# The 64-row products of an expansion placed beside the 64-row turns, whole-height state sums in the first group, and y times G on VectorE for the first two units

## The chip, the cores and the metric

The kernel runs on one core of a Trainium2 chip. The metric is the device time of one execution in microseconds. Before the change it is 840.27 us, the median of 3 runs (839.8 to 841.61); the profiled execution spans 840.4 us. All data are 32-bit floats.

## The reference

A linear-attention layer with a recurrent state is followed by a feed-forward block. The attention part runs over 4 batches x 8 heads x 768 steps with a head width of 40:

```python
for t in range(S):
    y[:, :, t] = einsum('bhd,bhde->bhe', r_t, state)
    Sa = einsum('bhde,bhe->bhd', state, a_t)
    state = state * w_t[:, :, None, :] - einsum('bhd,bhe->bhde', Sa, b_t) \
            + einsum('bhd,bhe->bhde', v_t, k_t)
```

Its output, read as 3072 tokens of width 320, goes through

```python
h = x @ w_in                      # 320 -> 2048
g = h * clip(h + 3, 0, 6) / 6
out = g @ w_out                   # 2048 -> 320
```

## The kernel before

The sequence is worked through in blocks of 64 steps. A *unit* is two batches of one such block, so there are 24 units; four units make a *group*. For each unit the kernel turns the inputs (transposes on TensorE), forms running products of the decay, solves a small triangular system (by an inverse that VectorE builds once a group, then small TensorE products), and updates the state: that is the scan. The finished output of a unit, `yg`, is moved by DMA into `xt`, laid out as two blocks of 128 features and one block of 64 features, the latter held twice, in rows 0 to 63 and in rows 64 to 127. The feed-forward block then runs on 128 tokens in two jobs per unit, each over half of the 2048 hidden features. In the first part of the run the 64-bit weights in HBM are also converted to 32 bits, by VectorE and ScalarE.

Programs of the engines are fixed when the kernel is built: a Python generator hands out the feed-forward work in *pieces*, which are put between the stages of the scan.

An expansion (320 features to 1024 hidden ones) fills two PSUM banks. Its first four pieces are products over 128 rows, and its fifth is the eight products over the last 64 features, in pairs that use rows 0 to 63 and rows 64 to 127:

```python
def expand(xt, j0, gts):
    hp = [bank("h", [P, NQ, P], 2) for _ in range(2)]
    for c in range(2):
        for t in range(2):
            for i in range(NQ):                                    # NQ = 4
                j = c * HJ + j0 + i
                nc.tensor.matmul(out=hp[c][:, i, :], lhsT=win[:, t, j * P:(j + 1) * P],   # L968
                                 rhs=xt[:, t, :], start=(t == 0 and i == 0), stop=False)
            yield True
    for i in range(NQ):
        for c in range(2):
            nc.tensor.matmul(out=hp[c][:, i, :],                                          # L973
                             lhsT=win2[half(c), (j0 + i) * P:(j0 + i + 1) * P],
                             rhs=xt[half(c), 2, :], start=False, stop=(i == NQ - 1))
    for c in range(2):
        gt = ffn.tile([P, NQ, P], F32, name="gt", bufs=5)
        nc.scalar.activation(out=gt[:], in_=hp[c][:], func=AF.Relu, ...)                  # L978
        nc.vector.scalar_tensor_tensor(out=gt[:], in0=gt[:], scalar=6.0, in1=hp[c][:], ...)  # L979
        gts.append(gt)
    yield True
```

The contraction of the job before follows in four pieces of two products each (16 of the profile's instructions in all), into one bank (`o`, L992). The generator alternates them:

```python
i, r = jobs.popleft()
gts = []
yield from expand(ready[i], r * NQ, gts)
if last:
    yield from contract(*last)
last = (i, r, gts)
```

The steady part of the scan issues the stages of several units together. `PRODUCTS` gives the order on TensorE: first the full 128-row turns `W`, `S`, `K`; then `RT`, `VT`, `A`, `B`, `factor`, which are *half turns* (64 rows by 128 columns, L430 and L570); then products on quarters of the array (64 rows by 64 columns):

```python
PRODUCTS = ["W", "S", "K", "RT", "VT", "A", "B", "factor",
            "y", "EV", "R", "C", "U", "UT", "rS", "sn", "H", "E", "F"]
TURNS = PRODUCTS[:3]
def together(stages):
    ...
    for name in PRODUCTS:
        for stage in stages.get(name, []):
            ...                       # the stage's TensorE part
    ...                               # then every stage's results
```

Two stages of the scan in detail. The new state is summed over 40 rows at a time, since a head has 40 rows in each half of the array:

```python
def s_sn():
    sn = ps_pair(NPR, D)
    ...
            nc.tensor.matmul(out=sn[q][half(s, D), pr, :],                                # L864
                             lhsT=o[name][half(q), h * D:(h + 1) * D], rhs=by, ...)
    yield PE
    for q in range(2):
        for s in range(2):
            x = st[half(s, D), q, :, 0:D]
            nc.vector.tensor_tensor(out=x, in0=sn[q][half(s, D)], in1=x, op=ALU.add)      # L873
```

The unit's output is multiplied by the running decay G. In the first two units (`fresh`: the state is still zero) there is nothing to add to it:

```python
def s_y():
    y = ps_pair(NPR, BL)
    ...                                                                                   # L888
    yield PE
    if fresh:
        m["ys"] = tmp.tile([P, NPR, 2, BL], F32, name="ys", tag="zs")
    for q in range(2):
        if fresh:
            nc.scalar.activation(out=m["ys"][:, :, q, :], in_=y[q], func=AF.Copy)         # L898
        else:
            nc.vector.tensor_tensor(out=m["ys"][:, :, q, :], in0=y[q],
                                    in1=m["ys"][:, :, q, :], op=ALU.add)                  # L900
    yg = m["yg"] = tmp.tile([P, NPR, P], F32, name="yg", tag="yg", bufs=2)
    nc.gpsimd.tensor_tensor(out=yg[:], in0=m["ys"]..., in1=o["G"][:], op=ALU.mult)        # L903
```

The tag `zs` is a single buffer; the triangular blocks (`third_block`) use it as well: ScalarE writes `zs` (L704) and TensorE reads it (L719).

Of the kernel before, what the change touches and what calls it, by code (L numbers as in the profile page):

```python
# [16 lines left out]
P = 128  # L17
BL = 64
HB = BL // 2
L = 32  # L20
SLOT = 64
# [8 lines left out]
def kernel(  # L30
# [42 lines left out]
    nc = tc.nc  # L73
    B, H, T, D = r.shape
    NG = T // (2 * BL)
    NPR = H // 2
    NP = B // 2
    NU = 2 * NP
# [16 lines left out]
    def bank(tag, shape, bufs):  # L95
        return ps.tile(shape, F32, name=tag, tag=tag, bufs=bufs)
# [11 lines left out]
    def ps_pair(*dims):  # L108

        n = 1  # L110
        for d in dims:
            n *= d
        if shared[0] is None or shared[1] + n > 512:
            shared[:] = [ps_any([P, 512]) for _ in range(2)], 0
        at = shared[1]
        shared[1] += n
        views, step = [], n
        for d in dims:
            step //= d
            views.append([step, d])  # L120
        return [_ap(t[:], at, views) for t in shared[0]]
# [6 lines left out]
        out=ident[:], in_=ones, pattern=[[1, P]],  # L128
# [4 lines left out]
        out=ones[:, 0:BL], in_=ones[:, 0:BL], pattern=[[1, BL]],  # L133
# [3 lines left out]
        out=ones[BL:P, 0:BL], in_=ones[BL:P, BL:P], pattern=[[1, BL]],  # L137
# [310 lines left out]
    def half(i, n=SLOT):  # L448
        return slice(SLOT * i, SLOT * i + n)
# [285 lines left out]
    def step(i):  # L735
# [117 lines left out]
                nc.scalar.activation(out=ys[:, rs::2], in_=ysp[rs], func=AF.Copy)  # L853

        def s_sn():
            sn = ps_pair(NPR, D)
            for name in "KB":
                for pr in range(NPR):
                    for s in range(2):
                        for q in range(2):  # L860
                            h = 2 * pr + s
                            by = VN[half(q), 4 * s + pr, 0:D] if name == "K" else \
                                m["U"][half(q), 4 * (s ^ q) + pr, 0:D]
                            nc.tensor.matmul(  # L864
                                out=sn[q][half(s, D), pr, :],
                                lhsT=o[name][half(q), h * D:(h + 1) * D], rhs=by,
                                start=(name == "K" and pr == 0), stop=(name == "B" and pr == NPR - 1),
                            )
# [11 lines left out]
        def s_y():  # L880
            y = ps_pair(NPR, BL)
            for name in "KB":
                for pr in range(NPR):
                    j, rs = pr // 2, pr % 2
                    for s in range(2):
                        for q in range(2):
                            h = 2 * pr + s
                            nc.tensor.matmul(  # L888
                                out=y[q][half(s), pr, :],
                                lhsT=o[name][half(q), h * D:h * D + SLOT],  # L890
                                rhs=m[name][half(q), 4 * rs + 2 * s + j, :],
                                start=(name == "K" and pr == 0), stop=(name == "B" and pr == NPR - 1))
            yield PE
            if fresh:
                m["ys"] = tmp.tile([P, NPR, 2, BL], F32, name="ys", tag="zs")
            for q in range(2):
                if fresh:
                    nc.scalar.activation(out=m["ys"][:, :, q, :], in_=y[q], func=AF.Copy)  # L898
                else:
                    nc.vector.tensor_tensor(out=m["ys"][:, :, q, :], in0=y[q],  # L900
                                            in1=m["ys"][:, :, q, :], op=ALU.add)
            yg = m["yg"] = tmp.tile([P, NPR, P], F32, name="yg", tag="yg", bufs=2)
            nc.gpsimd.tensor_tensor(out=yg[:], in0=m["ys"][:].rearrange("p r q t -> p r (q t)"),  # L903
                                    in1=o["G"][:], op=ALU.mult)

# [39 lines left out]
    def feed_forward():  # L945

        last = None
        while True:
            while not available():
                if last:  # L950
                    yield from contract(*last)
                    last = None
                yield None
            i, r = jobs.popleft()
            gts = []
            yield from expand(ready[i], r * NQ, gts)
            if last:
                yield from contract(*last)
            last = (i, r, gts)

    def expand(xt, j0, gts):

        hp = [bank("h", [P, NQ, P], 2) for _ in range(2)]
        for c in range(2):
            for t in range(2):
                for i in range(NQ):
                    j = c * HJ + j0 + i
                    nc.tensor.matmul(out=hp[c][:, i, :], lhsT=win[:, t, j * P:(j + 1) * P],  # L968
                                     rhs=xt[:, t, :], start=(t == 0 and i == 0), stop=False)
                yield True  # L970
        for i in range(NQ):
            for c in range(2):
                nc.tensor.matmul(out=hp[c][:, i, :],  # L973
                                 lhsT=win2[half(c), (j0 + i) * P:(j0 + i + 1) * P],
                                 rhs=xt[half(c), 2, :], start=False, stop=(i == NQ - 1))
        for c in range(2):
            gt = ffn.tile([P, NQ, P], F32, name="gt", bufs=5)
            nc.scalar.activation(out=gt[:], in_=hp[c][:], func=AF.Relu, bias=three[:], scale=1.0)  # L978
            nc.vector.scalar_tensor_tensor(out=gt[:], in0=gt[:], scalar=6.0, in1=hp[c][:],  # L979
                                           op0=ALU.min, op1=ALU.mult)  # L980
            gts.append(gt)
        yield True

    def contract(i, r, gts):
        split = i < SPLIT
# [292 lines left out]

    m = 0
    for i in range(NU, NK):  # L1280
        for j in range(BLOCKS):
            rate, inversion = 3.5, 0
            if i + AHEAD >= NK + NU - 1:
                rate = 4.5
            if i < 2 * NU - 1:
                rate = 2.8
            parts = a_block(m)
            next(parts)
            if side or i % NU == NU - 1 and rate < 4:
# [12 lines left out]
            m += 1  # L1302
# [36 lines left out]
```

## Time and profile before

| | |
|---|---|
| time, median of 3 | 840.27 us |
| TensorE (PE), matmuls | 753.9 us busy, 90% |
| VectorE (DVE) | 549.1 us, 65% |
| ScalarE (ACT) | 322.6 us, 38% |
| GpSimd (POOL) | 158.2 us, 19% |
| mean granted TensorE clock | 0.937 |
| PE busy, 330 to 760 us | 100, 99.02, 100 and 59.97 us in the stretches 400-500, 500-600, 600-700 and 700-760; 70 of 70 us in 330-400 |
| PE busy, 60 to 150 us | 33.55 of 60, then 20.99 of 30 us |
| DVE busy, 60 to 150 us | 47.99 of 60, then 23.56 of 30 us |

In the profile each 32-bit product stands as two TensorE instructions: the 768 products at L968 are 1536 there. They are pipelined and overlap, so what one costs is read from start to start, and not from its own duration. A form such as `64*128` gives the rows and columns of the array that an instruction uses.

### The profile page before, as it was taken

How to read it: one execution, taken by the hardware profiler on the slowest of the kernel's cores; microseconds unless marked ns; L12 is line 12 of the kernel's file. 1: busy time of each engine (PE TensorE's matmuls, PEld its weight loads, DVE VectorE, ACT ScalarE, POOL GpSimd, SP SyncE). 2: the span in 40 equal slices, each digit the busy share in tenths (PEclk: the TensorE clock that was granted, in tenths of full speed). 3: DMA queues.
4: the chain of work that ended last, by engine and by line, in shares of the span. 5: the costliest groups of instructions: out<-in, count | busy, mean ns of one | idle time of the engine just before them, and what ended most of it. 6: DMA issues, size and time to landing. Idle time of an engine off the chain costs nothing.

```text
span 840.4 us, 35835 instructions
## 1 busy us (share of the span) xinstructions
PE 753.9 (90%) x15832; PEld 635.5 (76%) x15832; DVE 549.1 (65%) x1112; ACT 322.6 (38%) x868; POOL 158.2 (19%) x307
## 2 busy tenths in 40 slices
PE   4722866898999998999999999999999999999998
PEld 3622766686877877888888888888888888888886
DVE  6989597887865769855589744699556675232211
ACT  1322654232265533454433545334553324322111
POOL 3231310222112230312230322022122102000000
PEclk9755576999999998999999999999999999999999
DMA  7573343331033331232321332231232101110000
GB/s 140 83 176 92 90 105 91 69 68 34 9 59 59 63 61 28 43 55 46 61 44 33 59 59 44 44 57 29 47 64 43 24 22 28 25 23 15 16 19 16
DMA packets 174218, 45.05 MB, mean 54 GB/s; under 512 B 157424, under 2 KB 172784, under 8 KB 174064
## 3 DMA queue, kind: packets, MB, share of 16 engines
q1 hardware_dynamic: 171920, 42.44, 25.7%
q8 instruction: 125, 2.05, 1.0%
q10 hardware_dynamic: 2144, 0.33, 0.2%
q14 instruction: 29, 0.24, 0.1%
HBM read 34.08 MB, written 3.93 MB: 45 GB/s over the span
## 4 chain that ended last, share of the span: by engine, by line
PE 73%; DVE 12%; issue 6%; ACT 2%; POOL 2%; DMA 2%; SPq 0%; POOLq 0%; DVEq 0%; ACTq 0%
PE o L992 23%; PE h L968 20%; PE h L973 5%; PE any L458 4%; PE any L888 3%; PE any L420 2%; PE any L430 2%; PE any L864 2%; PE any L770 1%; DVE prod L660 1%; PE any L809 1%; DVE parts L320 1%; DVE x L666 1%; PE any L830 1%; DVE score L467 1%
## 5 line engine op out<-in xcount | busy, mean ns | idle before, releaser
L992 PE MATMUL o<-wout,gt 128*128 128x320 f32 x768 | 234.6, 449 | 0.0
L968 PE MATMUL h<-xt,win 128*128 128x128 f32 x1536 | 198.1, 283 | 5.0 <-DVE gt L979 5.0
L968 PEld LDWEIGHTS h<-xt,win 128*128 128x128 f32 x1536 | 186.7, 196 | 13.9 <-DVE gt L979 5.7
L992 PEld LDWEIGHTS o<-wout,gt 128*128 128x128 f32 x768 | 139.3, 191 | 54.4 <-issue 1.4
L979 DVE SCALAR_TENSOR_TENSOR gt<-gt,h 128x512 f32<-128x512 f32 x96 | 61.3, 681 | 87.1 <-ACT gt L978 87.0
L978 ACT ACTIVATE gt<-h,three 128x512 f32<-128x512 f32 x96 | 60.8, 684 | 108.3 <-PE h L973 108.2
L903 POOL TENSOR_TENSOR yg<-ys,gam 128x512 f32<-128x512 f32 x24 | 41.4, 1726 | 182.9 <-DVE ys L900 125.5
L660 DVE TENSOR_TENSOR prod<-x 128x30 f32<-128x30 f32 (+9 forms) x180 | 61.9, 344 | 13.5 <-POOL x L651 8.1
L590 POOL TENSOR_TENSOR KBt<-K,rgt 128x320 f32<-128x320 f32 x24 | 21.2, 882 | 248.2 <-ACT rgt L580 213.2
L666 DVE TENSOR_TENSOR x<-x,prod 128x30 f32<-128x30 f32 (+9 forms) x180 | 63.3, 352 | 5.2
L873 DVE TENSOR_TENSOR state<-any,state 40x160 f32<-40x160 f32 x96 | 30.9, 321 | 47.5 <-PE any L458 26.0
L973 PE MATMUL h<-xt,win 64*128 64x128 f32 x768 | 55.8, 285 | 0.0
L467 DVE COPY_PREDICATED score<-mask,any 128x256 f32<-128x256 int32 x143 | 53.4, 437 | 1.7 <-PE any L458 1.1
L973 PEld LDWEIGHTS h<-xt,win 64*128 64x128 f32 x768 | 46.6, 187 | 5.2 <-issue 0.3
L495 DVE RECIPROCAL gam<-prods 128x256 f32<-128x256 f32 x24 | 41.5, 1741 | 13.4 <-POOL yg L903 12.1
L510 DVE RECIPROCAL rgam<-prods 128x256 f32<-128x256 f32 x24 | 41.8, 1741 | 0.0
L484 DVE TENSOR_TENSOR_SCAN prods<-wm,start 128x528 f32<-128x528 f32 x24 | 30.1, 1254 | 17.5 <-ACT wm L481 15.8
L623 ACT ACTIVATE EV<-any 64x160 f32<-64x160 f32 x92 | 24.9, 297 | 43.0 <-PE any L617 34.7
L888 PE MATMUL any<-score,KBt 64*64 64x64 f32 x1536 | 31.8, 233 | 3.5 <-DVE score L467 2.1
L888 PEld LDWEIGHTS any<-score,KBt 64*64 64x64 f32 x1536 | 27.9, 145 | 6.4 <-issue 2.4
L900 DVE TENSOR_TENSOR ys<-any,ys 128x256 f32<-128x256 f32 x44 | 16.6, 419 | 24.4 <-PE any L617 12.6
L749 ACT ACTIVATE RT<-any 128x256 f32<-128x256 f32 (+1 forms) x44 | 15.5, 401 | 42.4 <-PE any L430 42.4
(195 smaller groups left out, 1107.2 us busy)
## 6 DMA issues: line engine op xcount, KB each, us to landing
B<-in_b_dram SPq DMA_DIRECT2D x48, 80.0 KB
K<-in_k_dram SPq DMA_DIRECT2D x48, 80.0 KB
V<-in_v_dram SPq DMA_DIRECT2D x96, 40.0 KB
out_dram<-ob SPq DMA_DIRECT2D x48, 80.0 KB
R<-in_r_dram SPq DMA_DIRECT2D x92, 40.0 KB
W<-in_w_dram SPq DMA_DIRECT2D x40, 80.0 KB
A<-in_a_dram SPq DMA_DIRECT2D x40, 80.0 KB
xt<-yg SPq DMA_DIRECT2D x72, 40.0 KB
```

The source lines that it names most:

```text
L467: nc.vector.copy_predicated(out=x[:, 4 * i:4 * i + 4, :], mask=mask4, data=o[i])
L495: nc.vector.reciprocal(gv[:, :, 0:HB], o["prods"][:, :, 0, 1:HB + 1][:, :, ::-1])
L510: nc.vector.reciprocal(rv[:, :, HB:BL], o["prods"][:, :, 1, 1:HB + 1])
L660: nc.vector.tensor_tensor(out=pv, in0=_ap(x[:], (i + 1) * L + i, [[L, n], [0, i]]), in1=_ap(x[:], i * L, [[0, n], [1, i]]), op=ALU.mult,)
L666: nc.vector.tensor_tensor(out=rest, in0=rest, in1=pv, op=ALU.add)
L888: nc.tensor.matmul(out=y[q][half(s), pr, :], lhsT=o[name][half(q), h * D:h * D + SLOT], rhs=m[name][half(q), 4 * rs + 2 * s + j, :], start ...
L903: nc.gpsimd.tensor_tensor(out=yg[:], in0=m["ys"][:].rearrange("p r q t -> p r (q t)"), in1=o["G"][:], op=ALU.mult)
L968: nc.tensor.matmul(out=hp[c][:, i, :], lhsT=win[:, t, j * P:(j + 1) * P], rhs=xt[:, t, :], start=(t == 0 and i == 0), stop=False)
L973: nc.tensor.matmul(out=hp[c][:, i, :], lhsT=win2[half(c), (j0 + i) * P:(j0 + i + 1) * P], rhs=xt[half(c), 2, :], start=False, stop=(i == N ...
L978: nc.scalar.activation(out=gt[:], in_=hp[c][:], func=AF.Relu, bias=three[:], scale=1.0)
L979: nc.vector.scalar_tensor_tensor(out=gt[:], in0=gt[:], scalar=6.0, in1=hp[c][:], op0=ALU.min, op1=ALU.mult)
L992: nc.tensor.matmul(out=op[:], lhsT=gts[c][:, n, :], rhs=wout[:, c * HJ + r * NQ + n, :], start=((split or r == 0) and c == 0 and n == 0), ...
```

## The change

It has three parts.

1. The eight 64-row products of an expansion no longer have to be its fifth piece. From unit 7's turn on (`spread`), they are held back or drawn forward: `together` issues them ahead of the first half turn (or, where a stage has no half turn, ahead of the first of its narrow products). If no such place has come by then, they go out after the third piece of the contraction that follows. The results (L978, L979 before) are issued as soon as both the 128-row and the 64-row products have been. As an expansion is then four pieces instead of five, the rate of pieces is multiplied by 8/9.
2. In the first group (units 0 to 3), the state's products take 64 columns of the weights instead of 40, so that all 128 rows of `sn` are written, and VectorE adds two 128-row tiles instead of four 40-row ones. The extra rows are not used later.
3. For the first two units VectorE multiplies `y` by `G` straight from PSUM, in two instructions; ScalarE's two copies and GpSimd's multiplication go, and so does the use of the buffer `zs`.

```diff
         def s_sn():
+            wide = SLOT if i < NU else D
...
-                                out=sn[q][half(s, D), pr, :],
-                                lhsT=o[name][half(q), h * D:(h + 1) * D], rhs=by,
+                                out=sn[q][half(s, wide), pr, :],
+                                lhsT=o[name][half(q), h * D:h * D + wide], rhs=by,
...
-                for s in range(2):
-                    x = st[half(s, D), q, :, 0:D]
-                    nc.vector.tensor_tensor(out=x, in0=sn[q][half(s, D)], in1=x, op=ALU.add)
+                for rows in [slice(0, P)] if i < NU else [half(s, D) for s in range(2)]:
+                    x = st[rows, q, :, 0:D]
+                    nc.vector.tensor_tensor(out=x, in0=sn[q][rows], in1=x, op=ALU.add)
...
+            yg = m["yg"] = tmp.tile([P, NPR, P], F32, name="yg", tag="yg", bufs=2)
             if fresh:
-                m["ys"] = tmp.tile([P, NPR, 2, BL], F32, name="ys", tag="zs")
+                for q in range(2):
+                    nc.vector.tensor_tensor(out=yg[:, :, half(q)], in0=y[q], in1=o["G"][:, :, half(q)],
+                                            op=ALU.mult)
+                return
...
+    narrow, spread, LATEST = [], [False], 2
...
             if last:
-                yield from contract(*last)
+                for n, x in enumerate(contract(*last)):
+                    if n == LATEST and narrow:
+                        narrow[0]()
+                    yield x
+            if narrow:
+                narrow[0]()
...
+        def short():
+            narrow.clear()
+            for i in range(NQ):
+                for c in range(2):
+                    add(c, i, win2[half(c), (j0 + i) * P:(j0 + i + 1) * P], xt[half(c), 2, :])
+            if begun[0] + begun[1] == 6 * NQ:
+                results()
...
+        narrow.append(short)
         for c in range(2):
             for t in range(2):
                 for i in range(NQ):
...
+                if c == 1 and t == 1 and not narrow:
+                    results()
                 yield True
...
+        if not spread[0] and narrow:
+            short()
+            yield True
...
-        owed[0] += n
+        owed[0] += n * (8 / 9 if spread[0] else 1)
...
+    FIRST_NARROW = PRODUCTS[len(TURNS)]
...
         for name in PRODUCTS:
+            if name == FIRST_NARROW and narrow and spread[0] and stages:
+                narrow[0]()
...
     for i in range(NU, NK):
+        spread[0] = i >= 2 * NU - 1
```

More of the change, by code (lines that the diff above doesn't have):

```diff
@@ L893, in s_y @@
             yield PE
+            yg = m["yg"] = tmp.tile([P, NPR, P], F32, name="yg", tag="yg", bufs=2)
             if fresh:
-                m["ys"] = tmp.tile([P, NPR, 2, BL], F32, name="ys", tag="zs")
+                for q in range(2):
+                    nc.vector.tensor_tensor(out=yg[:, :, half(q)], in0=y[q], in1=o["G"][:, :, half(q)],
+                                            op=ALU.mult)
+                return
             for q in range(2):
[L897 to L902, printed above, removed]
+                nc.vector.tensor_tensor(out=m["ys"][:, :, q, :], in0=y[q],
+                                        in1=m["ys"][:, :, q, :], op=ALU.add)
             nc.gpsimd.tensor_tensor(out=yg[:], in0=m["ys"][:].rearrange("p r q t -> p r (q t)"),
@@ L963, in expand, with add, results @@
         hp = [bank("h", [P, NQ, P], 2) for _ in range(2)]
+        begun = [0, 0]
+        def add(c, i, lhsT, rhs):
+            nc.tensor.matmul(out=hp[c][:, i, :], lhsT=lhsT, rhs=rhs, start=(begun[c] == 0),
+                             stop=(begun[c] == 3 * NQ - 1))
+            begun[c] += 1
+        def short():
[5 more added lines that the diff above has]
+                results()
+        def results():
+            for c in range(2):
+                gt = ffn.tile([P, NQ, P], F32, name="gt", bufs=5)
+                nc.scalar.activation(out=gt[:], in_=hp[c][:], func=AF.Relu, bias=three[:], scale=1.0)
+                nc.vector.scalar_tensor_tensor(out=gt[:], in0=gt[:], scalar=6.0, in1=hp[c][:],
+                                               op0=ALU.min, op1=ALU.mult)
+                gts.append(gt)
+        narrow.append(short)
         for c in range(2):
@@ L967, in expand @@
                     j = c * HJ + j0 + i
-                    nc.tensor.matmul(out=hp[c][:, i, :], lhsT=win[:, t, j * P:(j + 1) * P],
-                                     rhs=xt[:, t, :], start=(t == 0 and i == 0), stop=False)
+                    add(c, i, win[:, t, j * P:(j + 1) * P], xt[:, t, :])
+                if c == 1 and t == 1 and not narrow:
+                    results()
                 yield True
[L971 to L982, printed above, removed]
+        if not spread[0] and narrow:
+            short()
+            yield True
     def contract(i, r, gts):
```

## The prediction

> **What bounds the kernel now.** I read the 40 slices first, then the chain that ended last, then windows of TensorE's timeline.
>
> ```profile
> PE   4722866898999998999999999999999999999998
> DVE  6989597887865769855589744699556675232211
> ...
> PE 73%; DVE 12%; issue 6%; ACT 2%; POOL 2%; DMA 2%; SPq 0%; POOLq 0%; DVEq 0%; ACTq 0%
> ```
>
> There are two regimes. Until about 157 us (slice 7) TensorE is half idle and VectorE is the fullest engine; from there TensorE is full to the end. Adding the gaps between its records gives 18.7 us of idle time from 88 to 157 us, 6.3 from 157 to 250, 5.5 from 250 to 330, and only 1.2 from 330 to 840. So after 330 us everything taken off TensorE's sequence comes off the time, and nothing done to another engine does. But "busy" there doesn't mean at its best rate, as the timeline of a stretch shows:
>
> ```profile
> 515.33 1.34 PE L992 MATMUL o<-wout,gt 128*128 128x320 f32 x4
> 516.51 1.95 PE L968 MATMUL h<-xt,win 128*128 128x128 f32 x16
> 518.30 0.60 PE L420 MATMUL any<-ident,W 128*128 128x128 f32 x4
> 518.83 0.47 PE L430 MATMUL any<-ident,R 64*128 64x64 f32 x8
> ...
> 521.01 2.05 PE L968 MATMUL h<-xt,win 128*128 128x128 f32 x16
> 523.00 1.16 PE L973 MATMUL h<-xt,win 64*128 64x128 f32 x16
> 524.09 1.34 PE L992 MATMUL o<-wout,gt 128*128 128x320 f32 x4
> ```
>
> Sixteen wide products from 516.51 to 518.30 take 1.79 us (0.112 each) when the neighbours on both sides use 128 rows. The sixteen from 521.01 to 523.00, between a narrow block and the 64-row products, take 1.99. The 0.2 us is in the switches: in the records of single instructions the first step inside is 213 ns and not 112, and the last one, to L973, 205. L973 likewise: pairs come 112 ns apart, but the first pair takes 213, the last product is 201 ns from L992 where 105 would do, and L992's first step is 374, not 269. The sum for 64-row products alone among wide ones is 93 + 101 + 96 + 105 = 0.39 us. The end of the run confirms it:
>
> ```profile
> 813.39 3.73 PE L968 MATMUL h<-xt,win 128*128 128x128 f32 x32
> 817.05 1.16 PE L973 MATMUL h<-xt,win 64*128 64x128 f32 x16
> 818.15 4.57 PE L992 MATMUL o<-wout,gt 128*128 128x320 f32 x16
> 822.56 3.73 PE L968 MATMUL h<-xt,win 128*128 128x128 f32 x32
> ```
>
> A job takes 822.56 - 813.39 = 9.17 us, while 32 x 0.112 + 8 x 0.112 + 16 x 0.269 is 8.78.
>
> **What the Trainium skill says.** "TensorEngine Tiling (Array Packing)", Key Properties: changing the tiling mode, not just the tile, drains TensorE. The trace agrees: each change between `128*128`, `64*128` and `64*64` costs about 0.1 us on either side. The records from wide to half turn give 94 + 50 ns, from half turn to quarter product 122 on the step, from quarter product back to wide 133 + 101 to 111. A full turn followed by a wide product of the same form keeps the 109 ns step: turning as such is no switch. "TensorE: Matmul & The Clock Gate", LDWEIGHTS: a weight load takes time by its columns, not its rows. Agrees: L864 with 40 columns steps by 10 ns, L809 with 64 and the same 40 moving elements by 14. "VectorE: DVE Perf Modes", First, the fixed hardware budget: each of the 128 partitions is a lane. So adding 128 rows should last as long as adding 40; the trace has no 128-row twin of L873, but L775, 128x160 from PSUM, took 316 ns against its 321.
>
> **Part 1, the 64-row products.** I counted neighbours in the order of TensorE's instructions in the two programs, 48 blocks each. Before, 33 stand alone among 128-row instructions, 12 follow quarter products and precede wide ones, and 3 precede quarter products. After, 27 stand directly ahead of half turns (15 behind a full turn, 10 behind wide products, 2 behind a contraction), 8 alone, 2 behind quarter products and 11 ahead of them. What one adds in switches:
> - alone: 0.39 us (0.35 where a full turn follows);
> - between quarter and wide products: 242 + 201 - 244 (the switch that is there anyway) = 0.20;
> - between wide and quarter products: 194 + about 130 - 115 = 0.21, where 130 is my estimate from the 122 of half turns to quarter products;
> - ahead of half turns: the entry costs 194, but the half turns no longer pay theirs of 144, and the step between the two is of one form, `64*128`. With 20 ns for that (a half turn to the next one steps by 29 above its pace), 0.07 us.
>
> Before: 33 x 0.38 + 12 x 0.20 + 3 x 0.21 = 15.6 us. After: 8 x 0.39 + 27 x 0.07 + 2 x 0.20 + 11 x 0.21 = 7.7. That takes off 8 us, nearly all of it after 290 us where TensorE is the bound. The arithmetic itself stays.
>
> **Its price.** With no stages left at the end, three blocks go out after the third contraction piece, and only four instructions (4 x 0.269 + 0.105 = 1.18 us) lie between them and the next use of what they release.
>
> ```profile
> 827.31 8.88 PE L992 MATMUL o<-wout,gt 128*128 128x320 f32 x32
> 827.41 1.27 ACT L978 ACTIVATE gt<-h,three 128x512 f32<-128x512 f32 x2 [4.17 <-PE h L973]
> 828.14 1.28 DVE L979 SCALAR_TENSOR_TENSOR gt<-gt,h 128x512 f32<-128x512 f32 x2 [7.88 <-ACT gt L978]
> ```
>
> The first bank is free at 828.14 + 0.64, which is 1.5 us after the 64-row products gave way at 827.31; TensorE waits some 0.35 us, three times: +1 us. In the scan, stages lie between the forced place and the next expansion, so I give later results only +0.7 us: the wait for L979 was 1.0 us in all after 330 us.
>
> **Parts 2 and 3, the start.** All four first state sums are pieces of the chain (90.1, 103.2, 126.6, 153.9 us). Each loses two of four adds: 4 x 2 x 0.321 = 2.6 us. The first y:
>
> ```profile
> 98.69 1.08 PE L719 MATMUL any<-zs,tt 32*32 32x32 f32 x64
> 99.92 0.66 ACT L898 ACTIVATE ys<-any 128x256 f32<-128x256 f32 x2 [2.87 <-PE any L719]
> 100.65 1.29 POOL L903 TENSOR_TENSOR yg<-ys,gam 128x512 f32<-128x512 f32 x1 [10.14 <-ACT ys L898]
> 101.89 0.21 POOL L755 TENSOR_TENSOR scale<-last,dec 128x8 f32<-128x8 f32 x1
> 102.14 0.49 DVE L757 TENSOR_TENSOR state<-state,scale 128x320 f32<-128x320 f32 x1 [4.37 <-POOL scale L755]
> ```
>
> The product y ended at 97.7, but ScalarE's copy waited for L719, a reader of the shared `zs` buffer; the small `scale` stood behind the long multiplication in GpSimd's queue, and VectorE waited 4.4 us for it. Afterwards VectorE multiplies at 97.7 (2 x 0.4 us, by L900's 419 ns), does L299 and L307 (0.36 + 0.61) and could scale the state at 99.6. The next state sum then waits for TensorE's L864, which no longer waits 0.6 us for the copies, and starts near 101.2 and not 103.15. The balance by 157 us: 1.9 here, 2.6 from the sums, -0.8 for the second unit's multiplication on VectorE, and -0.5 for wider weights (64 x 4 ns = 0.26 us a unit, partly on the path) = 3.2. I count 2.5, as parts of this chain run over ScalarE and a TensorE at half clock (0.56 granted from 60 to 120 us).
>
> **Sum.** 840.3 - 8.0 - 2.5 + 1.0 + 0.7 = 831.5 us.
>
> **Rivals.**
> *The step from 64-row products to half turns is a switch too.* The one is a multiplication, the other a transpose. For: no record before has this pair. Against: in the 128-row form the two mix at 109 ns. It would cost 27 x about 0.15 to 0.2 = 4 to 5 us of the 8: 836.
> *VectorE or a PSUM bank becomes the bound in the middle.* VectorE is 73% busy from 400 to 600 us and runs in order; each `gt` now stands ahead of a stage's results, 1.3 us of it, and a half turn comes 1.1 us later than before. Against: the scan's products after the turn (0.5 to 1.5 us) cover that, and TensorE waited 1.2 us in 510. If each of some 40 blocks lost 0.15 us, +6: 837.
> *The early gain is hidden.* From 198 to 320 us there are waits of several us behind the inverse and behind GpSimd's `KBt` and the loads that it releases. If these are timed by DMA and not by what TensorE finished, 2.5 us are lost: 834. They seem to hang on TensorE's order, so I leave half a chance.
>
> **Range and chances.** The first part is the largest and the best founded; its main uncertainty is the one unseen step, which only makes it worse. All going well is 828, two rivals at once 838. Range 827.5 to 837. Faster by over 2% would be below 823.5: 0.03. Slower by over 2%, above 857: 0.01.
>
> **What would show it.** Right: half turns 0.06 to 0.13 us behind the last 64-row product at full pace; wide runs closing at 112 ns more often; the block L973's mean step unchanged; after 330 us TensorE idle below 3 us, and that stretch about 7 us shorter; the state scaling near 99.6 us, with its 4.4 us wait gone; dense TensorE work beginning 2 to 3 us before 157. Wrong: a 0.2 us step from 64-row products to half turns; waits of L968 for `gt` growing past 3 us; the first job starting as late as before.

## The result and the profile after

| | before | after |
|---|---|---|
| time, median | 840.15 us (839.8 to 841.61, 4 runs) | 832.7 us (831.98 to 834.51, 4 runs) |
| ratio | | 0.9911, 95% interval 0.9892 to 0.9931 |
| span of the profiled execution | 840.4 us | 830.2 us |
| TensorE idle, 330 us to its last instruction | 1.0 us | 6.5 us |
| first wide product; first product of a contraction | 118.19; 151.71 us | 113.73; 145.75 us |

The change takes off 0.9%, 7.5 us, and 831.5 was predicted. The total is right by luck: the start gave twice what was forecast, and the 64-row products a quarter to a third of their forecast.

The slices and the chain that ended last, after:

```profile
PE   4732877898999999999999999999999999999997
DVE  7999697988964769844589654799556685232201
...
PE 70%; DVE 12%; issue 9%; ACT 3%; POOL 2%; DMA 1%; SPq 0%; POOLq 0%; DVEq 0%; ACTq 0%
```

The digits look as before, but TensorE's share of the chain has fallen from 73 to 70% and "issue" has risen from 6 to 9%: more of the chain is time in which an engine waits for nothing that the profile shows.

The step that no record of before had, in the timeline after:

```profile
422.20 1.16 PE L974 MATMUL h<-xt,win 64*128 64x128 f32 x16
423.20 0.41 PE L430 MATMUL any<-ident,R 64*128 64x64 f32 x8
423.44 0.42 PE L430 MATMUL any<-ident,V 64*128 64x64 f32 x8
423.79 1.16 PE L889 MATMUL any<-score,KBt 64*64 64x64 f32 x64
```

From 422.20 to 423.20 is 1.00 us: eight pairs at 0.112 and one entry of 0.10. Nothing is left for a switch to the half turns; multiplication and transpose of one form follow each other at full pace. (L974, L990, L1015 and L865 are the lines L968/L973, L979, L992 and L864 of before.)

The three longest entries among the waits of TensorE from 322 us on (us in all, times, the longest), after:

```profile
PE h L974 <- DVE gt L990: 2.7, 4, 1.2
PE any L458 <- issue: 2.1, 3, 0.8
PE any L696 <- ACT wm L481: 1.3, 1, 1.3
```

Before, the same view had a single line, `L968 <- DVE gt L979` with 1.0 us. This is where the gain of the middle went. The end of the run, after:

```profile
802.19 3.84 PE L974 MATMUL h<-xt,win 128*128 128x128 f32 x32 [0.22 <-DVE gt L990]
...
809.19 1.16 PE L974 MATMUL h<-xt,win 64*128 64x128 f32 x16
810.28 1.34 PE L1015 MATMUL o<-wout,gt 128*128 128x320 f32 x4
811.84 3.84 PE L974 MATMUL h<-xt,win 128*128 128x128 f32 x32 [0.22 <-DVE gt L990]
```

The wait for a free PSUM bank behind the forced place was foreseen; it shows as 0.22 us of idle time and comes three times. A job takes 811.84 - 802.19 = 9.65 us, though, where it took 9.17 before: 0.48 us more. Matmuls overlap (a contraction product lasts 0.53 us and the next one begins after 0.27), so the profile counts TensorE as busy until the last one ahead of a wait has run out, and its idle time is less than the delay. And the start, where before the state was scaled at 102.14 us, 12.04 us after the first state sum of 90.10, and the second sum began at 103.15:

```profile
96.09 0.76 DVE L898 TENSOR_TENSOR yg<-any,gam 128x256 f32<-128x256 f32 x2 [2.45 <-PE any L889]
97.70 0.48 DVE L757 TENSOR_TENSOR state<-state,scale 128x320 f32<-128x320 f32 x1
98.75 0.56 DVE L874 TENSOR_TENSOR state<-any,state 128x160 f32<-128x160 f32 x2
```

After, the first sum is at 89.36 us, so the scaling follows it by 8.34 and the second sum by 9.39 (13.05 before). VectorE's wait for GpSimd is gone. Counting from the first sum takes out the start of a program, which differs between the profiled executions (the first sum is at 89.36 us here and at 90.46 in gamlate, a kernel that has parts 2 and 3 too).

### The profile page after: what moved, and what is told of

It is laid out like the page before. It is cut to its first block, busy times and chain, and to the rows that moved or that the text cites. A ratio compares the mean times of both kernels' runs of the same rounds, so it can differ in the third digit from the quotient of the medians.

```text
span 830.2 us, 35843 instructions
## 1 busy us (share of the span) xinstructions
PE 746.4 (90%) x15832; PEld 632.0 (76%) x15832; DVE 547.4 (66%) x1108; ACT 321.7 (39%) x864; POOL 156.1 (19%) x305
## 3 DMA queue, kind: packets, MB, share of 16 engines
q8 instruction: 125, 2.05, 1.0%
## 4 chain that ended last, share of the span: by engine, by line
PE 70%; DVE 12%; issue 9%; ACT 3%; POOL 2%; DMA 1%; SPq 0%; POOLq 0%; DVEq 0%; ACTq 0%
PE h L974 24%; PE o L1015 22%; PE any L458 4%; PE any L889 3%; PE any L420 2%; PE any L430 2%; PE any L865 2%; DVE prod L660 2%; DVE x L666 2%; PE any L770 1%; PE any L809 1%; DVE parts L320 1%; PE any L830 1%; PE any L846 1%; PE any L696 1%
## 5 line engine op out<-in xcount | busy, mean ns | idle before, releaser
L974 PE MATMUL h<-xt,win 128*128 128x128 f32 (+1 forms) x2304 | 252.8, 284 | 7.0 <-DVE gt L990 7.0
L974 PEld LDWEIGHTS h<-xt,win 128*128 128x128 f32 (+1 forms) x2304 | 232.5, 193 | 25.8 <-issue 8.8
L1015 PE MATMUL o<-wout,gt 128*128 128x320 f32 x768 | 232.8, 445 | 0.2 <-DVE gt L990 0.2
L1015 PEld LDWEIGHTS o<-wout,gt 128*128 128x128 f32 x768 | 139.0, 191 | 51.2 <-issue 1.4
L990 DVE SCALAR_TENSOR_TENSOR gt<-gt,h 128x512 f32<-128x512 f32 x96 | 61.5, 677 | 61.2 <-ACT gt L989 61.2
L904 POOL TENSOR_TENSOR yg<-ys,gam 128x512 f32<-128x512 f32 x22 | 39.1, 1778 | 167.9 <-DVE ys L902 121.9
L874 DVE TENSOR_TENSOR state<-any,state 40x160 f32<-40x160 f32 (+1 forms) x88 | 27.9, 321 | 62.7 <-PE any L865 36.3
L666 DVE TENSOR_TENSOR x<-x,prod 128x30 f32<-128x30 f32 (+9 forms) x180 | 65.2, 362 | 5.4
L467 DVE COPY_PREDICATED score<-mask,any 128x256 f32<-128x256 int32 x143 | 53.4, 436 | 4.0 <-PE any L458 3.6
L729 ACT ACTIVATE tinv<-any 32x256 f32<-32x256 f32 (+1 forms) x56 | 19.3, 344 | 28.9 <-PE any L719 28.1
L775 DVE TENSOR_TENSOR RR<-any,EV 128x160 f32<-128x160 f32 x44 | 12.2, 318 | 25.6 <-PE any L458 25.4
```

Of the source, the lines that this page charges most:

```text
L467: nc.vector.copy_predicated(out=x[:, 4 * i:4 * i + 4, :], mask=mask4, data=o[i])
L666: nc.vector.tensor_tensor(out=rest, in0=rest, in1=pv, op=ALU.add)
L974: nc.tensor.matmul(out=hp[c][:, i, :], lhsT=lhsT, rhs=rhs, start=(begun[c] == 0), stop=(begun[c] == 3 * NQ - 1))
L1015: nc.tensor.matmul(out=op[:], lhsT=gts[c][:, n, :], rhs=wout[:, c * HJ + r * NQ + n, :], start=((split or r == 0) and c == 0 and n == 0), ...
```

## The experiments

All ratios are to runs of the kernel before made beside them; the last column is (ratio - 1) x 840.2 us.

| run | what it is | median us | ratio, 95% interval | us |
|---|---|---|---|---|
| p1_only | part 1 alone | 839.21 | 0.9983 (0.9975 to 0.9992) | -1.4 |
| p23_only | parts 2 and 3 alone | 834.58 | 0.9936 (0.9922 to 0.9950) | -5.4 |
| p2_only | part 2 alone | 838.08 | 0.9964 (0.9952 to 0.9977) | -3.0 |
| p3_only | part 3 alone | 838.7 | 0.9978 (0.9970 to 0.9986) | -1.8 |
| alone | changed kernel, 64-row products between wide ones | 843.53 | 1.0034 (1.0019 to 1.0050) | +2.9 |
| gamtail | changed kernel, reciprocal later, old order at the end | 828.68 | 0.9869 (0.9851 to 0.9888) | -11.0 |
| gamlate | changed kernel, reciprocal later | 830.78 | 0.9878 (0.9859 to 0.9896) | -10.3 |
| gam_p23 | parts 2 and 3, reciprocal later | 835.77 | 0.9935 (0.9915 to 0.9955) | -5.5 |
| shift32 | changed kernel, 128 idle instructions more on TensorE | 834.83 | 0.9940 (0.9926 to 0.9955) | -5.0 |
| shift64 | the same, 256 | 841.91 | 1.0012 (0.9999 to 1.0024) | +1.0 |
| ys_own | kernel before, `ys` out of the shared buffer | 845.51 | 1.0051 (1.0038 to 1.0063) | +4.3 |
| early_spread | gamtail, spread from the scan's first block on | 840.26 | 0.9994 (0.9982 to 1.0005) | -0.5 |

### The two halves apart: p1_only and p23_only

p1_only takes parts 2 and 3 out of the changed kernel; p23_only takes out part 1 with one line, so that the 64-row products are always the fifth piece:

```diff
     for i in range(NU, NK):
-        spread[0] = i >= 2 * NU - 1
```

> Part 1 alone: the 64-row products beside half turns; state sums and y as before. Theory (the switches are saved, and part of that is given back in new waits after 330 us): 840.2 - 8 + 4.5 = 836.5 us, TensorE idle 4 to 7 us after 330 us. Rival (the whole gain is the start): 840 us. Rival (the switches give all of the 7.5 us): 832.5 us.

> Parts 2 and 3 alone: whole state sums in the first group and y times G on VectorE, the 64-row products as the fifth piece, as before. Theory: 836.5 us (3 to 4.5 us less than before, all of it gained by 157 us and kept). Rival (the early gain is hidden later): above 839 us. Rival (it is all of the gain): 832.5 us.

Part 1 alone gives 1.4 us and was expected to give 3.7; parts 2 and 3 give 5.4, with 3 to 4.5 expected. The traces separate work and waiting, from the 128th instruction of the contractions (at 257 to 266 us) to TensorE's last, and from the 176th (at 325 to 336 us):

| | from the 128th: length | idle | busy | from the 176th: length | idle | busy |
|---|---|---|---|---|---|---|
| before | 569.8 | 6.3 | 563.5 | 500.4 | 1.0 | 499.4 |
| p1_only | 568.0 | 12.7 | 555.4 | 502.2 | 8.0 | 494.2 |
| p23_only | 569.9 | 6.2 | 563.7 | 500.4 | 1.0 | 499.5 |
| after | 565.8 | 10.9 | 554.9 | 500.3 | 6.5 | 493.7 |
| gamtail | 563.3 | 8.5 | 554.8 | 496.6 | 3.9 | 492.7 |
| gamlate | 566.0 | 9.8 | 556.2 | 499.2 | 5.2 | 494.0 |

From the 128th on, part 1 takes 8.1 us (8.8 on top of parts 2 and 3) off TensorE's busy time. That looks like the 8.0 that were worked out, but 3.0 of it come ahead of the 176th, where only two blocks have moved. The clock is the reason for most of that. The same products and the wait ahead of them, before and after:

```profile
319.37 1.31 PE L770 MATMUL any<-state,at 40*64 40x40 f32 x29 [3.69 <-DVE score L467]
320.52 1.16 PE L458 MATMUL any<-RT,VT 40*64 40x64 f32 x31
```

```profile
312.74 0.94 PE L770 MATMUL any<-state,at 40*64 40x40 f32 x29 [0.73 <-DVE score L467]
313.55 0.68 PE L458 MATMUL any<-RT,VT 40*64 40x64 f32 x31
```

Before, the granted clock is 0.50 for 6.8 us from 318.4 us on; after, it is full here. All six kernels with the 64-row products as the fifth piece have such a window, beginning between 310 and 322 us, and these 31 products take 1.15 or 1.16 us; in after, p1_only, gamtail, gamlate and shift32 they take 0.67 or 0.68. The work from 319.37 to 326.19 us lasted 6.8 us; at the steps of the full clock it would last about 4.2 (1.42 for the quarter products, as after, and 24 x 0.112 + 0.1 for the wide ones), so by this estimate the window costs 2.6 us. It begins as TensorE resumes after a wait of 3.7 us, which is short after the change; that the wait brings it about is not shown.

From the 176th on the clock is full in all six rows. There part 1 gains nothing in the changed kernel (500.4 and 500.3 us) and loses 1.8 us by itself. It takes 5.2 to 5.7 us off the busy time, and 5.5 to 7.0 come back as idle time. Read from start to start, as the overlap demands, both are larger: stops of TensorE delay it by 1.1 us before and by 8.2 after (the step across each stop less the usual step of such a pair). Without its stops the stretch would be 7.3 us shorter after than before.

### Is it the switches? alone

The 64-row products come after the first piece of the next contraction, so between 128-row instructions wherever no stage falls there, and parts 2 and 3 stay:

```diff
-    narrow, spread, LATEST = [], [False], 2
+    narrow, spread, LATEST = [], [False], 0
...
-            if name == FIRST_NARROW and narrow and spread[0] and stages:
-                narrow[0]()
```

> As the changed kernel, with its rate of 8/9, but the 64-row products are never drawn to a stage: they go out after the first piece of the contraction, alone among 128-row products. Theory (the placing beside half turns is what saves): every one of some 45 blocks costs 0.39 us of switches again, 45 x 0.38 = 17 us in place of 7.7, so 832.7 + 9 = 841.5 us, less 2 to 4 us of waits that come with the placing: 837.5 to 841. Rival (the new rate and the later results make the gain, not the neighbours): 833 us.

It is 10.4 us above the changed kernel by the ratios, and above the 837.5 to 841 expected: the waits that were to go were replaced by others (5.5 us for `gt` from 322 us on). Its trace has a window of half clock too, at 342 to 349 us. From the 208th instruction of the contractions on (357 and 365 us), where the clock is full in both, the busy time is 471.7 us against 463.4 in the changed kernel, and idle time is 3.9 against 5.2: the difference lies in the sequence and not in waits. The rate of 8/9 is the same in both, so what stands beside the same 64-row products sets their cost.

### Whose results come late: gamtail, gamlate, gam_p23

The longest wait of the middle, in the timeline after:

```profile
427.31 2.15 POOL L904 TENSOR_TENSOR yg<-ys,gam 128x512 f32<-128x512 f32 x1 [5.01 <-DVE ys L902]
427.95 1.24 ACT L989 ACTIVATE gt<-h,three 128x512 f32<-128x512 f32 x2
429.50 1.75 DVE L495 RECIPROCAL gam<-prods 128x256 f32<-128x256 f32 x1 [1.10 <-POOL yg L904]
431.17 1.22 DVE L990 SCALAR_TENSOR_TENSOR gt<-gt,h 128x512 f32<-128x512 f32 x2
431.95 1.13 PE L974 MATMUL h<-xt,win 128*128 128x128 f32 x8 [1.15 <-DVE gt L990]
```

ScalarE began `gt` at 427.95, and VectorE could have taken it up some 0.7 us later (the distance at 810 us is 0.72). But in its queue the reciprocal of `gam` stood first, and that one waited until 429.5 for GpSimd's multiplication and then took 1.75 us itself. TensorE needed the bank and stood for 1.15. The Trainium skill, "Perfetto Trace Analysis", says in the section on the Tensor Engine Instruction of ScalarE, VectorE and GpSimd that they are strict FIFO; the trace agrees: `gt` could be taken up from about 428.65, and VectorE, idle since 428.40, stood until 429.50 before an instruction ahead of it (1.10 us). Part 1 makes the order: the 64-row products were drawn at 422.20 with a wide piece (425.33) still to come, and the results come after that piece, no longer ahead of the stage's results.

If this is the cause, it is enough to draw the reciprocal one stage later (gamlate). gamtail also has the old order for the last blocks:

```diff
-    AHEAD_STAGES = [["W", "gam"], ["A", "B"], ["F", "K"], ...
-    CLOSE_STAGES = [["W", "gam"], ["A", "B"], ["F", "K", "factor"], ...
+    AHEAD_STAGES = [["W"], ["gam", "A", "B"], ["F", "K"], ...
+    CLOSE_STAGES = [["W"], ["gam", "A", "B"], ["F", "K", "factor"], ...
...
+    spread[0] = False          # ahead of the loop that issues what is left; gamtail only
     while jobs or next(stream):
```

gam_p23 has the first edit in p23_only, as a control.

> The changed kernel with two more edits: the reciprocal that waits for GpSimd's yg is issued a stage later, so that the results of an expansion no longer stand behind it in VectorE's queue; and after the last stage the 64-row products are the fifth piece again. Theory (two waits of 1.15 us near 431 and 549 us come from that queue, and three of 0.22 us from the late place at the end): both kinds vanish, 832.7 - 2.3 - 0.7 = 829.7 us. Rival (the waits come from the expansion's results being drawn too near to the next use, whatever stands ahead of them): waits stay within 0.5 us of theirs, and the time at 832 us; later turns of A may then even wait for the reciprocal, and cost 1 to 3 us.

> The changed kernel with the later reciprocal alone, without the repair of the last three blocks. Theory: of the 4.0 us that both edits took off, 0.66 are the three waits of the last blocks, so this one is at 829.3 to 830; waits of TensorE for gt at 307, 431 and 549 us gone, the three of 0.22 us after 797 still there. Rival (the last blocks' order gives most of it): 831 to 832.

> The 64-row products where the kernel before has them, parts 2 and 3 of the change, and VectorE's reciprocal of gam drawn one stage later. Theory (the later reciprocal helps only because results of 64-row products drawn ahead of a stage stand behind it in VectorE's queue): without those products ahead of stages there is nothing to free, so 834.6 as without the edit, at most 0.5 us off. Rival (a later reciprocal is good by itself): it takes the same 2 to 3 us here, 832.

The same place in gamtail's timeline:

```profile
425.63 2.15 POOL L904 TENSOR_TENSOR yg<-ys,gam 128x512 f32<-128x512 f32 x1 [5.00 <-DMA R<-in_r_dram]
426.96 1.29 DVE L990 SCALAR_TENSOR_TENSOR gt<-gt,h 128x512 f32<-128x512 f32 x2 [0.25 <-ACT gt L989]
428.95 1.05 PE L974 MATMUL h<-xt,win 128*128 128x128 f32 x8
```

`gt` follows ScalarE by 0.70 us and TensorE goes on without a wait. No line `L974 <- DVE gt` is left in its view of waits after 150 us. By the ratios gamlate is 2.8 us below the changed kernel and gamtail another 0.7. These are differences of medians of 4 or 5 runs, good to about 2 us: at the end of the run, where gamtail alone has the old order again, its jobs take 9.17 us and not 9.65, which is 1.4 us in three. gamlate's median, 830.78, lies above the 829.3 to 830 that the theory gave it and just below the rival's 831 to 832, so the split between the two edits is less uneven than forecast. The control, gam_p23, gained nothing (-5.5 against -5.4): a later reciprocal is of no use by itself. In its trace the one wait for `gt` that p23_only has (0.9 us at 549.6) is gone, and two new ones of 0.8 us are there instead. That one, like its fellow of 1.0 us at 558 us before, stands behind the same reciprocal, 1.10 us idle for GpSimd included; part 1 makes two of 1.15 us out of it. So the queue is the cause of these waits. gamtail is faster than both kernels.

The later reciprocal has a cost of its own: gamtail has a wait that the changed kernel has not, `L719 <- DVE score L467`, three times and 1.9 us in all; gamlate has it with 1.6 us, and in gam_p23 it makes up the 1.7 us of the two new ones. The traces give the edits less than the medians do: from the 128th instruction on, gamlate is as long as the changed kernel (566.0 and 565.8 us), and from the 176th on 1.1 us shorter; gamtail is 2.5 and 3.7 us shorter. That the two waits of 1.15 us can be had back is shown; that all of the gain in time comes from them is not.

### The waits that nobody ends: shift32 and shift64

Three times, near 362, 481 and 599 us, TensorE stops amid 64 quarter products, where the profile shows nothing that they wait for (after):

```profile
361.71 0.58 PE L458 MATMUL any<-RT,UT 40*64 40x64 f32 x25
363.06 0.28 PE L458 MATMUL any<-RT,UT 40*64 40x64 f32 x3 [0.77 <-issue]
```

The Trainium skill, "Runtime: NRT & Kernel Launch", Instruction fetch mechanics, says that an engine's instructions arrive in blocks of 256 (16 KiB), and that crossing into the next one is mostly hidden. The queue of instructions in the profile moved 2.05 MB in 125 packets, 16.4 KB each, and a packet lies near each of these stops. The stop at 362 us stands behind a dense stretch. If the blocks are the cause, 128 more instructions ahead must take the stops away from these products, and 256 must bring them back. At about 79 us, with results that nothing uses:

```diff
+    pads = [bank("h", [P, NQ, P], 2) for _ in range(2)]
+    for n in range(32):                                  # 64 in shift64
+        nc.tensor.matmul(out=pads[n % 2][half(0), 0, 0:SLOT], lhsT=ident[half(0), 0:SLOT],
+                         rhs=ident[half(0), 0:SLOT], start=True, stop=True)
```

> As the changed kernel, with 32 small products (128 TensorE instructions with their weight loads) put in near 79 us, where TensorE waits for the inverse. Nothing reads them. Theory (the three waits of 0.6 to 0.8 us near 362, 481 and 599 us, at instructions that stand 4096 and 5376 apart, are TensorE's instruction stream arriving late in a dense stretch, so they depend on where its blocks begin): they vanish or move to other products, and the time changes by -2 to +1 us. Rival (they wait for another engine's result): the same three waits stay at the same products, with the same length.

> The changed kernel with 64 products of 64x64 put in at about 79 us, whose results nothing uses: 256 of TensorE's instructions with their weight loads, against 128 in the run with 32 products. Theory (the three waits of 0.6 to 0.8 us in the quarter products near 362, 481 and 599 us are those of an instruction stream that arrives 256 instructions at a time): with a shift by a whole 256 the limits between packets fall on the same products again, so the three waits come back, 0.6 to 0.8 us each, after the same products; time 833 to 835. Rival (any shift of the program's timing takes these waits away): they stay away, as with 128.

The same stretch with 128 more instructions (shift32), and the stops with 256 more (shift64):

```profile
363.82 0.63 PE L458 MATMUL any<-RT,UT 40*64 40x64 f32 x28
364.24 0.22 PE L458 MATMUL any<-at,kt 40*64 40x64 f32 x1
```

```profile
363.08 2.70 PE L974 MATMUL h<-xt,win 128*128 128x128 f32 x29 [0.59 <-issue]
368.60 0.28 PE L458 MATMUL any<-RT,UT 40*64 40x64 f32 x4 [1.32 <-issue]
```

With 128 more, all three stops are gone, and smaller ones stand elsewhere (0.35 at 490, 0.49 at 503 and 0.41 us at 572). With 256 more, the stop at 362 is back within one instruction of the same product (TensorE's 6263rd matmul after, 6390th with 128 matmul records more), now of 1.32 us; the second is back likewise (8913th and 9040th), with 0.78; the third is not. The new one of 0.59 us, at the 6264th matmul, is 126 matmuls ahead of the 6390th, with their weight loads 252 records: about one block earlier. Other kernels with part 1 agree: p1_only stops within four matmuls of all three, though it gets there 6 us later, and gamtail and gamlate stop at the first and the third. So that these stops go with the place in the instruction stream is shown, and that a shift of 256 brings them back, for two of three. Where such a limit falls is an accident of the program's order, and part 1 changed the order: the kernel before had no stop of this kind after 330 us.

The times of the two runs say nothing of this: the extra products delay the start. The first state scaling is at 99.2 us with 32 products and 104.8 with 64 (97.7 after), and TensorE ends 1.5 and 4.9 us later. Why shift64's median lies another 5 us above its profiled execution (836.85 us) was not found.

### The start: p2_only, p3_only, ys_own

> Part 2 alone: the first group's state sums over 128 rows. Theory (each of four sums on the chain loses 0.65 us, and the wider weights take back up to 0.3 us each at half clock): 838.5 to 839.5 us, against 840.2 before. Rival (the sums are most of the early gain of 5.6 us): 836 us.

> Part 3 alone: y times G by VectorE for the first two units. Theory (it is the larger part of the early gain: the 4.4 us wait before the state's scaling goes): 836 to 837.5 us. Rival (part 3 only trades ScalarE's and GpSimd's work for VectorE's, with 1 us or less to gain): 839.3 us or more.

Part 2 gives 3.0 us, more than the 0.7 to 1.7 expected, and part 3 gives 1.8, less than the 2.7 to 4.2 expected; together 4.8, where both in one kernel gave 5.4. From the first state sum to the second there are 13.05 us before, 12.09 with part 2, 10.25 with part 3, 9.72 with both and 9.39 after. p1_only, with the old start, has 12.95.

ys_own asks what of VectorE's 4.4 us was due to the shared buffer. In the kernel before:

```diff
-                m["ys"] = tmp.tile([P, NPR, 2, BL], F32, name="ys", tag="zs")
+                m["ys"] = tmp.tile([P, NPR, 2, BL], F32, name="ys", tag="yg", bufs=2)
```

> The kernel before, with one word changed: the copies of the first two units' y go to a buffer of yg's and not to the one that the triangular blocks use. ScalarE still copies and GpSimd still multiplies. Theory A (the wait was the shared buffer): the copies run near 98 us and not 99.9, and some 2 us of part 3's gain come with that alone: 838 us. Theory B (it was GpSimd's long multiplication ahead of the small one): the wait of VectorE falls from 4.4 to about 2.5 us, and the time by less than 1 us: 839.3 to 840.2 us.

The waits from 86 to 115 us in ys_own:

```profile
POOL yg L903 <- DMA xt<-yg: 12.9, 1, 12.9
DVE state L757 <- POOL scale L755: 8.4, 2, 6.2
```

As a test of time it is a miss: two buffers now serve `ys` and `yg`, and the second unit's multiplication waits 12.9 us for the first one's `yg` to be moved. Only the first unit can be read: counted from the first state sum, the copies come 2.2 us earlier (7.65 for 9.82 us behind it), and VectorE's first wait for `scale` falls from 4.4 to 2.2 us. In that unit the buffer was half of the wait, and the rest stayed with the copies and GpSimd's long multiplication still there. Taking all of it out, as part 3 does, was the better repair.

### Spreading from the beginning: early_spread

```diff
-        spread[0] = i >= 2 * NU - 1
+        spread[0] = True
```

> Both edits, and the 64-row products spread from the first block of the scan on instead of from the third group. Theory (the switches are paid for by the bound engine only, and before 290 us TensorE waits for others anyway): 0 to 0.5 us off 828.7, as one more block goes ahead of a half turn and eleven ahead of quarter products become twelve. Rival (early blocks delay results on the chain of the inverse): 0.5 to 1.5 us slower, with longer waits of TensorE before 330 us.

10.5 us slower than gamtail by the ratios: all of its lead is lost, far more than the rival allowed. The waits from 250 to 350 us:

```profile
PE h L974 <- DMA xt<-yg: 3.0, 1, 3.0
PE any L617 <- issue: 1.8, 1, 1.8
```

From 88 us to its last instruction TensorE is idle 38.0 us in early_spread and 28.9 in gamtail, which is 9.1 of the 11.3 us between the two profiled spans. The scan falls behind between two scalings of the state: they are at 245.2 and 272.1 us in gamtail, at 246.3 and 278.6 here. In between TensorE stands for a token block whose `xt` hasn't landed. The lag is never made up, and `L696 <- ACT wm L481` then costs 1.1 to 1.9 us in three groups. So the start of the spreading at unit 7 matters. Whether the earlier products or the changed rate of pieces pushed the job ahead of its data wasn't separated.

## Why the prediction was right, and where it wasn't

**What bounds the kernel** held: after 330 us TensorE's own sequence and its waits were all that moved. (Its idle time there, read as 1.2 us, is 1.0.)

**Part 1, switches: right.** From the 176th instruction of the contractions on there are 36 of the 48 blocks. At the prediction's own costs they pay 26 x 0.38 + 10 x 0.20 = 11.9 us before and 25 x 0.07 + 8 x 0.21 + 3 x 0.39 = 4.6 after, so 7.3 should go; 7.3 went, without the stops (7.1 in p1_only, 8.0 in gamtail). The unseen step, given 0.02 us, shows none. Rival (a), a switch between multiplication and half turn, is false.

**Its price: this step failed.** "In the scan, stages lie between the forced place and the next expansion, so I give later results only +0.7 us" should read +4.9 in idle time (from 330 to 797 us, 1.0 in p23_only and 5.9 after) or +6.3 (1.0 before, 7.4 in p1_only). With the 1.0 forecast for the end the whole price was 1.7; measured as delay it is 8.2 - 1.1 = 7.1 us, as much as the switches saved, and the prediction's own sign, that the stretch after 330 us becomes about 7 us shorter, failed: from the 176th on it became 0.1 us shorter. The step asked whether TensorE's work covers ScalarE and VectorE at their usual pace, and so it does. It did not ask what stands ahead of `gt` in VectorE's queue at that moment: two waits of 1.15 us are behind a reciprocal which itself waits for GpSimd. The wait of 1.0 us that the prediction had seen was already one of this kind. Three stops of 0.6 to 0.8 us go with the instruction stream, which the prediction did not look at, and 1.3 us is one wait for ScalarE's `wm`, which is gone with the later reciprocal. These sum to 5.7; less the 1.0 us for `gt` that went, they make the 4.9 within 0.2. For the end the step was right and its size was not: 0.35 us a job was forecast, and a job grew by 0.48.

Rival (b), VectorE or a bank as the bound in the middle, was right in its amount (+6) and in the bank, and wrong in its form: not 0.15 us in each of 40 blocks but a few waits of about a microsecond, two of the kinds not due to VectorE. An average share of busy time, 73%, could not have shown that.

**Parts 2 and 3: right in mechanism, mis-sized.** 2.5 us was counted and 5.4 measured (4.2 to 6.6). Term by term:
- "4 x 2 x 0.321 = 2.6 us" for the sums. Four narrow adds take 1.34 us, two wide ones 0.56, as the second starts 0.24 us behind the first where narrow ones step by 0.33. That is 0.78 a sum, 3.1 in four. p2_only measured 3.0 (1.9 to 4.0), so it can't tell this from 2.6 - 0.5 for the wider weights.
- "could scale the state at 99.6": 9.5 us after the first sum; p3_only has 9.24. But "the next state sum then waits for TensorE's L864, ... and starts near 101.2", 1.6 later, was wrong: it starts 1.01 us later, as before the change. Part 3 brings 2.8 us between the two sums, and not 1.9.
- "-0.8 for the second unit's multiplication on VectorE" was counted in full. After, VectorE waits for y's products before both multiplications (2.8 us, 2.5 in the first), so part of it at least fell into idle time.
- Last, 3.2 was cut to 2.5 for ScalarE and the half clock, with no number behind it.

With 3.1, 2.8 and -0.5 the sum is 5.4. That it fits so exactly is more than the interval can support, and p3_only by itself kept 1.8 of its 2.8.

**Rival (c), the early gain hidden: false.** p23_only starts its contractions 7.8 us earlier than before (143.95 for 151.71), and keeps 8.6 us to the end (827.56 for 836.20). Both are more than the 5.4 of the medians: the runs before that were made beside it span 838.4 us in the median, 2.0 less than the profiled one, and p23_only's profiled span is 0.9 below its median.

**The sum.** Predicted -6.3 for part 1 and -2.5 for the start; measured for part 1 -1.4 alone, or -2.1 as the difference of the changed kernel to p23_only (whose intervals leave about 2 us either way), and for the start -5.4. The two errors of some 4 and 3 us cancel.

**Open.** By the traces part 1 on top of the others gains 4.1 us after the 128th contraction instruction, by the medians only 2.1. Of the 4.1 us, 4.0 lie ahead of the 176th, and the window of half clock that is gone there is worth some 2.6 of them. So what part 1 gained in time is in the main not the switches, whose gain the stops used up; whether part 1 keeps the clock up, through the shorter wait ahead of it, was not tested. The profiled execution after was also 1.8 us behind p23_only's at the first contraction already (145.75 and 143.95 us), ahead of all that part 1 moves, and I can't say if that is chance or belongs to the kernel. Nor is the cause known of a stop of 3.2 us at L617, between 190 and 206 us, in all kernels.

## What to carry to other kernels

Put instructions of one array form side by side, multiplication or transpose alike; count the neighbours and you have the gain in the sequence. Then follow each result that you moved into the queue of the engine that finishes it, and look at what stands ahead of it there and what that waits for: an idle VectorE can be the bound if the head of its queue waits. Measure a stop of TensorE from start to start, as its idle time shows less than the delay, and look at the granted clock before you put a shorter busy time down to an edit. And test the parts one by one even where the total came out as predicted.

## What the runs showed of the hardware

- A switch of form costs about 0.1 us on a side, and none is due between 64-row products and half turns of the same form: eight pairs take 0.90 us + 0.10 for the entry.
- A stop of TensorE costs 0.07 to 0.22 us more than its idle time shows: 0.22 us of idle time behind contraction products came with a step of 0.65 us where 0.27 is usual.
- TensorE can stop for 0.6 to 1.3 us with no engine in the profile that it waits for, in a stretch of quarter products, at the same places of its instruction stream in several kernels; 128 idle instructions far ahead took three such stops away, and 256 brought two back.
- Two back-to-back VectorE adds of 128 rows take 0.56 us, four of 40 rows 1.34, though a single one of either lasts 0.32.
